# One weight load split over two DMA queues: the first 16 rows of w_in go to ScalarE's queue

## The chip, the core and the metric

The kernel runs on one core of one Trainium2 chip. The metric is device time in microseconds (us) of one execution. A core has five engines that run side by side: TensorE (PE, matrix products), VectorE (DVE), ScalarE (ACT), GpSimd (POOL) and SyncE (SP). SP, ACT and POOL can start DMA transfers, each on a queue of its own; the transfers of all queues are carried out by the same 16 DMA engines. Data is worked on in SBUF, a memory of 128 rows (partitions).

## What is computed

All data is fp32. With x of shape (2, 1, 512), the reference computes, cut to what matters:

```python
xn = layernorm(x)
# A: attention of one new token over the last W = 4096 of 32768 cached positions
q = (xn @ wq)                      # 512 -> 32 heads x 128
s = softmax(q k^T / sqrt(128)) v   # 8 key/value heads, each used by 4 query heads
s = s @ wo                         # 4096 -> 512
# B: a gated MLP
z = gelu(xn @ w_in)                # 512 -> 1792
h = z[:896] * (layernorm(z[896:]) * w_sp + b_sp)
g = silu(h @ w_out)                # 896 -> 512
out = x + s * g
```

With a batch of 2 and one token, nearly all the work is reading: 89.4 MB of weights and cache go through SBUF once.

## The kernel before

**Staging.** The large inputs arrive in tiles of 128 SBUF rows. w_in (512 x 1792) is laid out as 128 rows of 4 x 1792 numbers, so one SBUF row receives 28,672 contiguous bytes; w_out gives 14,336 bytes per row; each half of wq, and each of the eight k and eight v tiles (one per key/value head, both batch items), gives 32,768. The tile `win` (w_in), the two wq halves and all k and v tiles, later wo, share a ring of four slots (pool `ring`, function `slot`): a load into a slot has to wait until the tile that was there has been used. `wout` and the small tiles have space of their own.

**Queues.** Every large load is issued by SP, in the order w_in, w_out, wq, wq, k0, k1, v0, k2, v1 and so on up to wo. ACT's queue carries `xs` (x as 2 rows, for the layernorm), the two scalars w_sp and b_sp (tile `wb1`) and, at the end, the output. POOL's queue carries x once more, for the last addition. Instructions of each engine run in the order in which they are written (class `InOrder`); a planner adds the waits. It hands the completions of the SP and ACT transfers to eight semaphores in turn (called DMAHW0 to DMAHW7 below), so a transfer can also wait for the one that was issued eight places before it.

**Compute at the start.** `xs` goes through the layernorm (`st`, `mv`, `va`, `rs`, `xn`) on DVE and ACT, is transposed on TensorE and copied to `xnT`. Then 16 products (`z<-win,xnT`, in two passes each) need all of `win` and `xnT`. After them come the queries (`q_ps<-wq,xnT`), in four steps as wq arrives, with the rest of the MLP between them. From then on each head needs its k tile (transposed on DVE into `kt`, then the products `s`), and one head later its v tile (products `acc`). The last loads are wo, used by the products `part` and `so`.

The lines of most instructions read L37 in the profile, since a helper issues them; tiles tell them apart.

Of the kernel before, what the change touches and what calls it, by code (L numbers as in the profile page):

```python
# [14 lines left out]
P = 128  # L15
# [27 lines left out]
def kernel(  # L43
# [14 lines left out]
    pe, dve, act, sp = (InOrder(tc, e) for e in (nc.tensor, nc.vector, nc.scalar, nc.sync))  # L58
# [6 lines left out]
    F = w_in.shape[1]  # L65
    FH = F // 2
    KT = D // P
# [17 lines left out]
    def slot(name, *shape):  # L85
        return ring.tile([P, *shape], F32, tag="slot", name=name)
# [2 lines left out]
        return ps.tile([P, *shape], F32, tag="kt", name=name, bufs=3)  # L89


    xs = sb.tile([B, D], F32, tag="p", name="xs", bufs=1)
    act.dma_start(xs, x[:, 0, :])
    win_v = w_in.rearrange("(p k) f -> p k f", p=P)
    win = slot("win", KT, F)
    sp.dma_start(win, win_v)
    wout = big.tile([P, FT, D], F32, tag="wout", name="wout")
    sp.dma_start(wout, w_out.rearrange("(p j) d -> p j d", p=P))
    wq_v = wq.rearrange("(p k) f -> p k f", p=P)
# [32 lines left out]
    for n in range(HKV):  # L132
        p = Unit()
# [460 lines left out]
```

## Time and profile before

| | before |
|---|---|
| three timed runs, median (lowest to highest) | 217.18 us (216.87 to 217.79) |
| the profiled execution: span from the first to the last instruction | 214.9 us |
| median less that span | 2.3 us |
| read from HBM | 89.40 MB, 416 GB/s over the span |
| DMA queue of SP (q1) | 4032 packets, 89.39 MB, 96.9% of the 16 DMA engines' span |
| DMA queue of ACT (q10) | 20 packets, 0.01 MB |
| busy: PE, DVE, ACT, POOL | 64%, 49%, 11%, 2% |

The record gives the profiled execution no time of its own beside the span, so the span stands for it; the 2.3 us to the median of the timed runs lie around it. A packet is one piece of a transfer that one DMA engine moves without a break; for the large loads it is one SBUF row. In a table by stretches of time, a packet is counted, with its whole duration and its bytes, in the stretch in which it starts; so the DMA share of a short stretch can exceed 1.

### The profile page before, as it was taken

How to read it: one execution, taken by the hardware profiler on the slowest of the kernel's cores; microseconds unless marked ns; L12 is line 12 of the kernel's file. 1: busy time of each engine (PE TensorE's matmuls, PEld its weight loads, DVE VectorE, ACT ScalarE, POOL GpSimd, SP SyncE). 2: the span in 40 equal slices, each digit the busy share in tenths (PEclk: the TensorE clock that was granted, in tenths of full speed). 3: DMA queues.
4: the chain of work that ended last, by engine and by line, in shares of the span. 5: the costliest groups of instructions: out<-in, count | busy, mean ns of one | idle time of the engine just before them, and what ended most of it. 6: DMA issues, size and time to landing. Idle time of an engine off the chain costs nothing.

```text
span 214.9 us, 2108 instructions
## 1 busy us (share of the span) xinstructions
PE 138.0 (64%) x862; PEld 43.4 (20%) x862; DVE 104.9 (49%) x161; ACT 23.9 (11%) x60; POOL 4.0 (2%) x20
## 2 busy tenths in 40 slices
PE   0172193835865983992594199089467759989873
PEld 0120021212111221220121023033111113432321
DVE  2604014079549549529608910985784387240301
ACT  5003003110001011021021002012100011030110
POOL 7000000000000000000000000000000000000000
PEclk9997578896597698599599559959966757996998
DMA  7999999999999999999999999999999999999990
GB/s 257 428 439 445 433 433 445 401 451 415 451 427 427 442 415 451 409 457 421 439 430 433 445 415 445 415 451 424 421 451 421 451 409 450 415 418 418 427 401 36
DMA packets 4092, 89.52 MB, mean 417 GB/s; under 512 B 486, under 2 KB 498, under 8 KB 884
## 3 DMA queue, kind: packets, MB, share of 16 engines
q1 hardware_dynamic: 4032, 89.39, 96.9%
q8 instruction: 6, 0.10, 0.2%
q14 instruction: 2, 0.02, 0.0%
q10 hardware_dynamic: 20, 0.01, 0.0%
q0 software_dynamic: 32, 0.00, 0.0%
HBM read 89.40 MB, written 0.00 MB: 416 GB/s over the span
## 4 chain that ended last, share of the span: by engine, by line
DMA 69%; DVE 14%; PE 12%; ACT 1%; issue 1%; SPq 1%; ACTq 0%; DVEq 0%
DMA k<-in_A_k_cache_dram 33%; DMA v<-in_A_v_cache_dram 27%; DVE kt L37 11%; DMA wo<-in_A_wo_dram 9%; PE acc L37 5%; PE s L37 4%; PE pp L37 2%; ACT p L37 1%; DVE pT L37 1%; SPq L37 1%; DVE sm L37 1%; DVE qw L37 1%; DVE res L37 0%; PE so L37 0%; DVE mg L37 0%
## 5 line engine op out<-in xcount | busy, mean ns | idle before, releaser
L37 DVE STREAM_TRANSPOSE kt<-k 128x2048 f32<-128x2048 f32 x32 | 72.5, 2285 | 1.4 <-DMA k<-in_A_k_cache_dram 1.3
L37 PE MATMUL acc<-v,pT 128*32 128x512 f32 x256 | 42.6, 825 | 11.6 <-DMA v<-in_A_v_cache_dram 10.2
L37 PE MATMUL s<-kt,qw 128*32 128x512 f32 x256 | 40.3, 683 | 5.7 <-DVE kt L37 4.2
L37 PE MATMUL pp<-p,swap 128*128 128x512 f32 x16 | 12.6, 880 | 20.0 <-ACT p L37 20.0
L37 DVE CUSTOM_DVE_ANT_1 sm<-s,own 128x512 f32<-128x512 f32 x8 | 5.5, 691 | 35.8 <-PE s L37 35.7
L37 PEld LDWEIGHTS acc<-v,pT 128*32 128x32 f32 x256 | 10.7, 156 | 42.1 <-issue 32.0
L37 PE MATMUL q_ps<-wq,xnT 128*32 128x512 f32 x64 | 10.5, 785 | 12.0 <-DMA wq<-in_A_wq_dram 12.0
L37 PEld LDWEIGHTS s<-kt,qw 128*32 128x32 f32 x256 | 10.6, 121 | 33.8 <-issue 19.5
L37 ACT ACTIVATE o<-acc,diag 128x128 f32<-128x128 f32 x30 | 8.7, 367 | 62.6 <-PE acc L37 62.2
L37 ACT ACTIVATE p<-sm,nb 128x512 f32<-128x512 f32 x8 | 5.8, 722 | 77.8 <-DVE nb L37 77.8
L37 PE MATMUL col<-o,selw 128*32 128x128 f32 (+1 forms) x28 | 7.6, 439 | 0.9 <-DVE o L37 0.9
L37 DVE TENSOR_TENSOR lsum<-pl,diag 128x4 f32<-128x4 f32 x3 | 0.5, 162 | 15.7 <-PE pl L37 15.7
L37 PE MATMUL z<-win,xnT 128*32 128x448 f32 x32 | 5.0, 794 | 4.5 <-DMA win<-in_B_w_in_dram 4.5
L37 DVE STREAM_TRANSPOSE pT<-pp 128x512 f32<-128x512 f32 x8 | 5.7, 713 | 4.3 <-PE pp L37 4.3
L37 PEld LDWEIGHTS pp<-p,swap 128*128 128x128 f32 x16 | 3.0, 235 | 20.7 <-ACT p L37 20.7
L37 PE MATMUL mo<-mg,same 128*128 128x16 f32 x16 | 3.2, 273 | 5.8 <-DVE mg L37 5.3
L37 PE MATMUL part<-wo,oT 128*32 128x512 f32 x48 | 5.9, 598 | 0.1
L37 ACT ACT_TABLE_LOAD x4 | 5.1, 1283 | 2.0 <-issue 1.9
L37 PEld LDWEIGHTS q_ps<-wq,xnT 128*32 128x32 f32 x64 | 2.0, 126 | 15.5 <-DMA wq<-in_A_wq_dram 12.2
L37 PE MATMUL xnT_ps<-ident,xn 2*128 2x2 f32 x4 | 0.6, 252 | 6.9 <-DVE xn L37 6.9
L37 PEld LDWEIGHTS mo<-mg,same 128*128 128x128 f32 x16 | 2.4, 188 | 12.2 <-DVE mg L37 12.2
L37 DVE STREAM_TRANSPOSE zt<-z 128x448 f32<-128x448 f32 x1 | 1.0, 978 | 7.8 <-ACT z L37 7.8
(110 smaller groups left out, 62.4 us busy)
## 6 DMA issues: line engine op xcount, KB each, us to landing
k<-in_A_k_cache_dram SPq DMA_DIRECT2D x8, 4096.0 KB, 23.6
v<-in_A_v_cache_dram SPq DMA_DIRECT2D x8, 4096.0 KB, 31.4
wq<-in_A_wq_dram SPq DMA_DIRECT2D x2, 4096.0 KB, 28.8
wo<-in_A_wo_dram SPq DMA_DIRECT2D x2, 2048.0 KB
win<-in_B_w_in_dram SPq DMA_DIRECT2D x1, 3584.0 KB, 11.2
wo<-in_A_wo_dram SPq DMA_DIRECT2D x3, 1024.0 KB, 21.2
wout<-in_B_w_out_dram SPq DMA_DIRECT2D x1, 1792.0 KB, 15.0
wo<-in_A_wo_dram SPq DMA_DIRECT2D x1, 512.0 KB, 25.3
```

The lines of the kernel that those rows point to most:

```text
L37: return self.tc.keep_in_program_order(call(*args, **kwargs))
```

## The change

The load of `win` is cut into two transfers into the same tile: rows 0 to 15 on ACT's queue, as ACT's first instruction, and rows 16 to 127 on SP's queue, as SP's first. The load of `xs`, which was ACT's first, comes second there.

```diff
+    FIRST = 16
+    win_v = w_in.rearrange("(p k) f -> p k f", p=P)
+    win = slot("win", KT, F)
+    act.dma_start(win[:FIRST], win_v[:FIRST])
+    sp.dma_start(win[FIRST:], win_v[FIRST:])
     xs = sb.tile([B, D], F32, tag="p", name="xs", bufs=1)
     act.dma_start(xs, x[:, 0, :])
-    win_v = w_in.rearrange("(p k) f -> p k f", p=P)
-    win = slot("win", KT, F)
-    sp.dma_start(win, win_v)
     wout = big.tile([P, FT, D], F32, tag="wout", name="wout")
     sp.dma_start(wout, w_out.rearrange("(p j) d -> p j d", p=P))
```

ACT's instructions at the start of the program, before (16x7168 is 16 rows of 7168 numbers; `wb` is the tile of the two scalars, `rtx` a step of the layernorm):

```order
L37 DMA xs<-in_A_x_dram 2x512
L37 DMA wb_83<-in_B_w_sp_dram 1x1
L37 DMA wb_83<-in_B_b_sp_dram 1x1
L37 ACT_TABLE_LOAD
L37 ACTIVATE rtx<-va 2x1 [waits DVE_49]
```

and with the change:

```order
L37 DMA win<-in_B_w_in_dram 16x7168
L37 DMA xs<-in_A_x_dram 2x512
L37 DMA wb_84<-in_B_w_sp_dram 1x1
L37 DMA wb_84<-in_B_b_sp_dram 1x1
L37 ACT_TABLE_LOAD
L37 ACTIVATE rtx<-va 2x1 [waits DVE_49]
```

One DMA stands ahead of what was there; the rest keeps its order. SP's instructions at the start, before:

```order
L37 DMA win<-in_B_w_in_dram 128x7168
L37 DMA wout<-in_B_w_out_dram 128x3584
L37 DMA wq_79<-in_A_wq_dram 128x8192
L37 DMA wq_81<-in_A_wq_dram 128x8192
L37 DMA k_89<-in_A_k_cache_dram 128x1x8192
L37 DMA k_91<-in_A_k_cache_dram 128x1x8192 [waits DMAHW1_49,DMAHW0_49,PE_49]
```

and with the change:

```order
L37 DMA win<-in_B_w_in_dram 112x7168
L37 DMA wout<-in_B_w_out_dram 128x3584
L37 DMA wq_80<-in_A_wq_dram 128x8192
L37 DMA wq_82<-in_A_wq_dram 128x8192
L37 DMA k_90<-in_A_k_cache_dram 128x1x8192 [waits DMAHW0_49]
L37 DMA k_92<-in_A_k_cache_dram 128x1x8192 [waits DMAHW1_49,PE_49]
```

The order is the same. With one transfer more among those that take the eight semaphores in turn, k0 is now the ninth, and its issue waits for the first transfer (DMAHW0), where it waited for nothing.

## The prediction, made before the changed kernel was run

> **What bounds the kernel now.** I began with the share of the DMA engines and the chain of work that ended last, both on the page of the profile.
>
> ```profile
> DMA  7999999999999999999999999999999999999990
> q1 hardware_dynamic: 4032, 89.39, 96.9%
> DMA 69%; DVE 14%; PE 12%; ACT 1%; issue 1%; SPq 1%; ACTq 0%; DVEq 0%
> ```
>
> The DMA engines are busy in 38 of 40 slices; 96.9% of their time over the span is SP's queue. Is that a stream without holes, or does it starve and recover? The table by stretches answers (last two columns: share of the 16 DMA engines, GB/s):
>
> ```profile
> 40.00:100.00 60.00, 40.28 (x226) 11.38 (x216) 38.43 (x39) 6.23 (x17) 0.00 (x0) 0.80 1.00 431
> 100.00:150.00 50.00, 32.49 (x200) 10.84 (x202) 28.68 (x31) 5.05 (x16) 0.00 (x0) 0.76 1.01 433
> 150.00:190.00 40.00, 30.30 (x159) 8.88 (x151) 23.89 (x29) 2.77 (x8) 0.00 (x0) 0.79 1.00 431
> ```
>
> From 40 to 190 us the share is 1.00. The stream never waits for compute, so the time is: when the DMA engines start, plus bytes at 431 GB/s, plus whatever holds them up, plus the tail. The chain, in order of time, shows both ends:
>
> ```profile
> 2.74 43.47 DMA k<-in_A_k_cache_dram
> 191.50 19.59 DMA wo<-in_A_wo_dram
> 211.13 0.47 PE so L37 x8
> ```
>
> Until 46.2 us the chain is the queue ahead of k0; at the end the last wo arrives at 211.09 and 3.8 us of tail follow. So a lag that one DMA engine picks up in the first microseconds is still there when its last packet lands: nothing downstream absorbs it, since each engine has its own share of every tile and the last one decides. The change moves no other byte, so it is to be priced in the first 12 us, in steps of 0.1 us:
>
> ```profile
> 1.60:1.70 0.10, 0.00 (x0) 0.00 (x0) 0.00 (x0) 0.00 (x0) 0.10 (x1) 1.00 0.10 41
> 1.70:1.80 0.10, 0.00 (x0) 0.00 (x0) 0.00 (x0) 0.00 (x0) 0.10 (x1) 1.00 3.57 860
> 1.80:1.90 0.10, 0.00 (x0) 0.00 (x0) 0.00 (x0) 0.00 (x0) 0.10 (x1) 1.00 3.42 860
> 1.90:2.00 0.10, 0.00 (x0) 0.00 (x0) 0.00 (x0) 0.09 (x1) 0.07 (x1) 1.00 3.10 860
> 2.00:2.10 0.10, 0.00 (x0) 0.00 (x0) 0.00 (x0) 0.10 (x1) 0.04 (x1) 1.00 2.14 573
> 2.10:2.20 0.10, 0.00 (x0) 0.00 (x0) 0.00 (x0) 0.10 (x1) 0.10 (x1) 1.00 0.88 287
> 2.30:2.40 0.10, 0.00 (x0) 0.00 (x0) 0.00 (x0) 0.10 (x1) 0.10 (x2) 1.00 0.75 287
> 2.40:2.50 0.10, 0.00 (x0) 0.00 (x0) 0.10 (x1) 0.10 (x1) 0.10 (x2) 1.00 1.03 287
> 2.50:2.60 0.10, 0.00 (x0) 0.00 (x0) 0.10 (x1) 0.10 (x1) 0.10 (x2) 1.00 0.76 287
> 2.70:2.80 0.10, 0.00 (x0) 0.00 (x0) 0.10 (x2) 0.10 (x1) 0.10 (x2) 1.00 0.67 287
> 4.60:4.70 0.10, 0.00 (x0) 0.00 (x0) 0.00 (x0) 0.10 (x1) 0.10 (x2) 1.00 2.66 1147
> ```
>
> One row of w_in is 28,672 bytes; in a 0.1 us step that is 287 GB/s. So 860 means three packets started there, 573 two, 1147 four. The share times 0.1 us times 16 engines is the time that those packets took. Up to 2.8 us 3+3+3+2+1+1+1+1+1 = 16 packets start, one per engine: the sixteen engines start spread over 1.0 us. Their time is 16.32 x 0.1 x 16 / 16 = 1.63 us each, while at 4.6 us a packet takes 2.66 x 1.6 / 4 = 1.06 us. The earlier one starts, the slower: the first twelve take 13.11 x 1.6 / 12 = 1.75 us, the last one 0.67 x 1.6 = 1.07. So the pace of an equal packet depends on what moves beside it.
>
> **The change part by part.** *The start.* The issues stand at the same place:
>
> ```profile
> 0.74 0.37 SPq L37 DMA_DIRECT2D win<-in_B_w_in_dram  x1
> 0.75 0.56 ACTq L37 DMA_DIRECT2D xs<-in_A_x_dram  x1
> ```
>
> ACT issues only 0.01 us after SP, so its queue starts nothing earlier than 1.7 us; the small xs of the 1.60 step is the earliest that its queue did. What can be won is the spread: 16 rows are one packet per engine, and if every engine then starts at 1.75 instead of at a mean of 33.0 / 16 = 2.06 (middles of the steps above), 0.31 us are won on average, at most 1.0 for the engine that started last. I take 0.31.
>
> *The pace.* The 128-row load is the one shape whose steady pace the trace shows. The change replaces it by 16 neighbouring rows, written by all 16 engines at once, and by 112 rows in sevens. No large transfer of before has such a shape. Lower bound: each of an engine's 8 packets keeps 1.06 us, no loss. Upper bound: writers into neighbouring rows go one after another, 16 x 1.06 = 17.0 us for the 16 rows, 16 us lost. The only transfer into few rows is xs, 2 rows by two engines at once: share 0.10 x 1.6 / 2 = 0.08 us for 2,048 bytes, which is full pace (28,672 bytes at 1.06 would be 0.076 per 2,048). It speaks for the lower end, though 14 times smaller than a row of w_in. The nearest row with full-size packets that meet is the crowd of the first twelve, 1.75 us. I take that, between ends far apart, for all 8 packets of an engine: 8 x (1.75 - 1.06) = 5.5 us, of which 0.57 (1.63 - 1.06, the first packet's surplus) is paid already: **+4.9 us**.
>
> [...]
>
> *x behind 16 rows.* xs now waits behind one packet on its two engines. How a small packet fares beside SP's stream, the DMA lines show for 5.9 to 6.0 us:
>
> ```profile
> DMA packets 7, 0.09 MB, mean 871 GB/s; under 512 B 3, under 2 KB 4, under 8 KB 4
> q10 hardware_dynamic: 1, 0.00, 0.6%
> ```
>
> That is the first packet of the scalar w_sp, issued at 1.34. So beside a full SP queue ACT's may be served only after four of SP's packets. In that bad case: own row from 5.9 to 7.0, then SP, own completion, SP, x at about 9, its completion 10.2. Who waits:
>
> ```profile
> 2.69 0.67 DVE L37 BATCH_NORM_STATS2 st<-xs 2x6 f32<-2x512 f32 x1
> 7.64 0.17 DVE L37 COPY xnT<-xnT_ps 128x8 f32<-128x8 f32 x1 [0.86 <-PE xnT_ps L37]
> 12.03 4.29 PE L37 MATMUL z<-win,xnT 128*32 128x448 f32 x24 [4.50 <-DMA win<-in_B_w_in_dram]
> 17.13 0.54 SPq L37 DMA_DIRECT2D k<-in_A_k_cache_dram  x1
> 25.88 3.64 PE L37 MATMUL q_ps<-wq,xnT 128*32 128x512 f32 x16 [8.49 <-DMA wq<-in_A_wq_dram]
> 46.23 2.31 DVE L37 STREAM_TRANSPOSE kt<-k 128x2048 f32<-128x2048 f32 x1 [1.34 <-DMA k<-in_A_k_cache_dram]
> ```
>
> From bn_stats to xnT are 5.1 us. x from 2.7 to 10.2 puts xnT at 15.3 and z 3.3 us later than 12.0 (nothing if w_in itself comes 4.9 later). z frees the slot of k1, issued at 17.13; its bytes are not due before k0's are through at 46.2. A cover of some 29 us, and 8.5 us ahead of the queries; cost 0. DVE and ACT are idle in between, and behind ACT's extra issue (about 0.5 us, as xs now) stand only the small loads and a table load that the layernorm needs after x.
>
> *k0's new wait.* SP now holds k0's issue, at 2.74 before, until the 16 rows are in; behind it stands k1, which waits for z anyway. Ahead of k0 are 3.67 + 1.84 + 8.39 = 13.9 MB, 32 us at 431 GB/s. Even 17 us leave half of that; cost 0. Without that cover each us would count whole.
>
> *Sum.* Against the span of 214.9: -0.31 + 4.9 = +4.6, span 219.5; with 2.3 us around it, or 217.18 + 4.6, **221.8 us**.
>
> **The rivals.**
>
> *Nothing changes (217.0).* The two pieces together write the same bytes to each row, both beside each other; if engines seldom meet, the pace stays 1.06 and 0.2 to 0.3 us of start is all. For it: xs at full pace; 431 GB/s as a limit of the engines themselves, whatever the rows. Against: the 1.75 us of the first crowd.
>
> *Faster (215.6).* If the spread of starts costs the last engine its 1.0 us and the surplus of 0.57 comes from that ragged start, both go: 217.18 - 1.57. Against: the earliest starters are the slowest, so a common start should make the crowd larger.
>
> *Much slower (225.1).* Two engines share each way into SBUF during all of w_in: every packet takes 2 x 1.06, 8 x 1.06 = 8.5 us, less the 0.57 paid: +7.9. It decides once engines meet in pairs all the time. For it: all 16 rows are neighbours; against: sevens lie apart, and engines drift.
>
> *The change doesn't do what it says:* ACT's 16 rows are served after four SP packets, as the scalar was. Then they don't start the stream at all, the start's 0.31 is lost and the crowding comes later: 222.1, no other sign.
>
> **How the numbers follow.** About 0.5% (1.1 us) is what a measurement can tell from no change. Forecast, with its late-served form: 0.40 (its own range 218.5 to 224). Much slower: 0.20. Nothing: 0.31. Faster: 0.09. Slower by over 0.5%: 0.40 + 0.20 = 0.60; same 0.31; faster 0.09. Cases of both signs are open, so the range reaches from 216.3 (part of the start won) to 227.5 (the paired price and 2 us of drift), leaving out about 0.08 below and 0.1 above, where neighbours serialise further.
>
> **What would show it.** After the change, steps of 0.1 us should show all 16 first packets by about 2.0 us, and packets of 28.7 KB at 1.5 us or more until w_in is in; z starting at 16 to 17 us; k0's issue after the 16 rows, at no price; the stretches from 40 to 190 us again at a share of 1.00 with the same tail, and the last wo later by what w_in was late. If the early packets take 1.06 us, the forecast is wrong and it is the first rival; if xnT comes after w_in, and the stretches behind show holes, the cover was misjudged.

## The result, and the profile after

The changed kernel takes 226.01 us (median of six runs, 224.89 to 227.29) against 217.55 for the kernel before (216.87 to 218.21, six runs): a ratio of 1.0394, 95% interval 1.0366 to 1.0422. By the ratio it is 8.6 us slower (the medians differ by 8.5). The profiled execution's span grew by 9.3 us, from 214.9 to 224.2.

The page of the changed kernel, its DMA share, bytes per slice and queues:

```profile
DMA  9998999999999999999999999999999999999980
GB/s 174 206 240 304 445 438 462 392 455 421 427 456 409 444 447 403 438 456 403 450 418 438 450 409 438 462 398 447 427 421 456 415 438 449 409 409 428 424 351 11
q1 hardware_dynamic: 4016, 88.93, 95.3%
q10 hardware_dynamic: 52, 0.47, 1.3%
```

The share says the DMA engines are as busy as ever. The second line says what they deliver: in the first four slices (5.6 us each) 174 to 304 GB/s, from the fifth on about 430, until the stream ends. The share alone would have hidden the whole loss: a packet that crawls counts as busy.

The stretch from 1.5 to 20.5 us, of the kernel before and then of the changed one (last columns: DMA share, GB/s):

```profile
1.50:20.50 19.00, 5.96 (x38) 2.26 (x38) 6.87 (x30) 4.18 (x7) 3.26 (x14) 0.97 1.01 423
```

```profile
1.50:20.50 19.00, 0.61 (x4) 0.55 (x4) 4.19 (x20) 2.97 (x4) 3.25 (x14) 1.00 1.00 228
40.00:100.00 60.00, 40.32 (x234) 12.16 (x230) 36.32 (x48) 7.10 (x18) 0.00 (x0) 0.77 1.01 434
150.00:190.00 40.00, 30.10 (x162) 8.41 (x164) 26.71 (x23) 3.91 (x12) 0.00 (x0) 0.82 1.00 432
```

By 20.5 us the changed kernel has fetched (423 - 228) x 19 us = 3.7 MB less; at the 431 GB/s of the rest of the stream that is 8.6 us, as much as the timed difference. From 40 us on the rate is what it was. When w_in was whole, the issue lines tell (last column: us from issue to landing), of the kernel before and then of the changed one, for SP's piece:

```profile
win<-in_B_w_in_dram SPq DMA_DIRECT2D x1, 3584.0 KB, 11.2
```

```profile
win<-in_B_w_in_dram SPq DMA_DIRECT2D x1, 3136.0 KB, 20.3
```

Both were issued at 0.74, so the last row of w_in lands 9.1 us later. The end of the changed kernel's chain of waits:

```profile
200.71 19.46 DMA wo<-in_A_wo_dram
220.17 0.04 issue
220.22 0.47 PE so L37 x8
```

The last wo is issued at 200.71 instead of 191.50 and lands after 19.46 us instead of 19.59, with 4.0 us of tail instead of 3.8. So the 9.1 us by which w_in was late are 9.2 us at the last issue and 9.3 at the end: the lag of the first 20 us was carried through. The bytes give 8.6: they are a mean over the 16 engines, and a load is whole only when its last packet has landed.

Inside that stretch, first the kernel before from 1.5 to 10.6 us (queue: packets, MB, share of 16 engines), then the changed kernel from 1.5 to 17.9 us and, for ACT's 16 rows, from 3.0 to 6.5 us:

```profile
q1 hardware_dynamic: 128, 3.67, 99.8%
```

```profile
q1 hardware_dynamic: 110, 3.15, 82.4%
...
q10 hardware_dynamic: 16, 0.46, 84.0%
```

Before, the 128 packets of w_in took 0.998 x 9.1 x 16 / 128 = 1.14 us each. After, SP's took 0.824 x 16.4 x 16 / 110 = 1.97 us and ACT's 0.840 x 3.5 x 16 / 16 = 2.94 us. An engine has eight of them: 7 x 1.97 + 2.94 = 16.7 us instead of 9.1, 7.6 us more on average.

### The profile page after: what moved, and what is told of

It reads as the page before. It is cut to its first block, busy times and chain, and to the rows that moved or that the text cites. A ratio compares the mean times of both kernels' runs of the same rounds, so it can differ in the third digit from the quotient of the medians.

```text
span 224.2 us, 2109 instructions
## 1 busy us (share of the span) xinstructions
PE 135.2 (60%) x862; PEld 42.6 (19%) x862; DVE 105.0 (47%) x161; ACT 23.9 (11%) x60; POOL 4.0 (2%) x20
## 4 chain that ended last, share of the span: by engine, by line
DMA 73%; PE 13%; DVE 11%; ACT 1%; issue 1%; ACTq 0%; DVEq 0%
DMA v<-in_A_v_cache_dram 40%; DMA k<-in_A_k_cache_dram 19%; DMA wo<-in_A_wo_dram 9%; DVE kt L37 8%; PE acc L37 7%; DMA win<-in_B_w_in_dram 5%; PE s L37 3%; PE pp L37 2%; ACT p L37 1%; DVE pT L37 1%; DVE sm L37 1%; DVE qw L37 1%; DVE both L37 0%; PE col L37 0%; DVE res L37 0%
## 5 line engine op out<-in xcount | busy, mean ns | idle before, releaser
L37 PE MATMUL acc<-v,pT 128*32 128x512 f32 x256 | 39.0, 763 | 13.4 <-DMA v<-in_A_v_cache_dram 12.0
L37 PE MATMUL s<-kt,qw 128*32 128x512 f32 x256 | 38.6, 645 | 4.7 <-DVE kt L37 4.0
L37 PE MATMUL pp<-p,swap 128*128 128x512 f32 x16 | 13.9, 965 | 20.1 <-ACT p L37 20.1
L37 PEld LDWEIGHTS s<-kt,qw 128*32 128x32 f32 x256 | 9.2, 117 | 32.8 <-issue 19.4
L37 DVE BATCH_NORM_STATS2 st<-xs 2x6 f32<-2x512 f32 x1 | 0.7, 682 | 11.0 <-DMA xs<-in_A_x_dram 11.0
```

The source lines that it names most:

```text
L37: return self.tc.keep_in_program_order(call(*args, **kwargs))
```

## Experiments

Two theories stood against each other. **Rows**: a load is slow when it covers fewer than the 128 SBUF rows, by which rows it writes. **Queues**: two queues that take turns on each DMA engine, with x behind the larger one, slow each other.

### Both pieces on one queue

```diff
-    act.dma_start(win[:FIRST], win_v[:FIRST])
+    sp.dma_start(win[:FIRST], win_v[:FIRST])
```

> Both pieces of w_in, 16 rows and then 112, on SP's queue; x first on ACT's queue as before. Theory R (rows): a load into fewer than 128 SBUF rows is slow by its shape, whichever queue carries it: packets of w_in at about 2 us as in the changed kernel (229 GB/s from 12 to 16 us), z at 20 to 21 us, time within 1 us of the changed kernel's 226.0. Theory Q (queues): the loss comes from ACT's packets being interleaved with SP's on each DMA engine and from x behind them: w_in at 1.06 us per packet, z at about 12 us, 217.0 to 218.0.

Measured: 224.68 us, ratio 1.0349 (1.0326 to 1.0372). Its start:

```profile
1.50:20.50 19.00, 1.45 (x12) 0.90 (x16) 4.64 (x21) 2.97 (x4) 3.26 (x14) 1.00 1.00 252
19.66 5.61 PE L37 MATMUL z<-win,xnT 128*32 128x448 f32 x32 [11.97 <-DMA win<-in_B_w_in_dram]
```

With one queue and x early, 7.6 of the 8.6 us remain. The queue theory falls. The run came out a little faster than the row theory expected (225 to 227, z at 20 to 21 us). It also shows the 16 rows with no other large load beside them, since they are first in the queue; from 1.5 to 2.5 us:

```profile
q1 hardware_dynamic: 16, 0.46, 304.5%
```

That is 3.045 x 1.0 x 16 / 16 = 3.05 us a packet, where the first sixteen of the kernel before took 1.63. About 1 us less than in the changed kernel was measured, but the two intervals overlap, so what the second queue adds is not settled.

### Two queues, cut by columns

```diff
-    act.dma_start(win[:FIRST], win_v[:FIRST])
-    sp.dma_start(win[FIRST:], win_v[FIRST:])
+    LEFT = F * KT // 8
+    win_f, win_vf = win.rearrange("p k f -> p (k f)"), win_v.rearrange("p k f -> p (k f)")
+    act.dma_start(win_f[:, :LEFT], win_vf[:, :LEFT])
+    sp.dma_start(win_f[:, LEFT:], win_vf[:, LEFT:])
```

> w_in again on two queues in the same proportion, but cut by columns: the first 896 of the 7168 numbers of each of the 128 rows on ACT's queue ahead of x, the other 6272 on SP's. Every transfer covers 128 rows. Theory R: no loss, 217.0 to 218.0, a packet of 25,088 bytes at about 0.93 us; w_in read at 430 GB/s or more once under way. Theory Q: two queues still share each engine, and x still stands behind 8 packets: about 224 to 226.

Measured: 217.36 us, ratio 1.0014 (0.9994 to 1.0034): the same time as before.

```profile
1.50:20.50 19.00, 3.06 (x20) 1.33 (x24) 4.65 (x21) 2.97 (x4) 3.26 (x14) 1.00 1.02 420
12.86 0.68 DVE L37 BATCH_NORM_STATS2 st<-xs 2x6 f32<-2x512 f32 x1 [10.08 <-DMA xs<-in_A_x_dram]
18.05 5.85 PE L37 MATMUL z<-win,xnT 128*32 128x448 f32 x32 [0.33 <-DVE xnT L37]
```

Same split of bytes over the same two queues, 420 GB/s in the first 20 us. And x arrives 10 us late, so that z waits for xnT and starts 6 us later than before: that costs nothing. Two queues and a late x are both free; the shape is not. Nor does a second queue at the start win anything.

### x ahead of the 16 rows

```diff
+    xs = sb.tile([B, D], F32, tag="p", name="xs", bufs=1)
+    act.dma_start(xs, x[:, 0, :])
     FIRST = 16
...
     sp.dma_start(win[FIRST:], win_v[FIRST:])
-    xs = sb.tile([B, D], F32, tag="p", name="xs", bufs=1)
-    act.dma_start(xs, x[:, 0, :])
```

> As the changed kernel, but x is issued on ACT's queue ahead of the 16 rows. bn_stats again at about 2.7 us instead of 13.7. If x's lateness is hidden behind w_in (the prediction's cover), the time is 226.0 within 1; if a part of the loss is the late layernorm, 224 or less. z should start when w_in is in, at 19 to 21 us.

Measured: 226.52 us, ratio 1.0425 (1.0382 to 1.0469). bn_stats starts at 2.69 again, and z waits for w_in alone:

```profile
2.81 24.42 SPq L37 DMA_DIRECT2D k<-in_A_k_cache_dram  x2
7.65 0.17 DVE L37 COPY xnT<-xnT_ps 128x8 f32<-128x8 f32 x1 [0.87 <-PE xnT_ps L37]
21.15 5.49 PE L37 MATMUL z<-win,xnT 128*32 128x448 f32 x32 [13.62 <-DMA win<-in_B_w_in_dram]
```

xnT is ready 13 us before it is of use, and the time is that of the changed kernel within the intervals. k0 is issued at 2.81 here, against 11.37 in the changed kernel, where it waits for the 16 rows: that wait costs nothing either. The 16 rows are served later here than in the changed kernel; ACT's queue from 5.5 to 9.5 us:

```profile
q10 hardware_dynamic: 16, 0.46, 83.1%
```

They take 0.831 x 4.0 x 16 / 16 = 3.32 us each, so a later turn does not make them faster.

### The 112 rows alone

```diff
-    act.dma_start(win[:FIRST], win_v[:FIRST])
...
+    nc.gpsimd.memset(win[:FIRST], 0.0)
```

> The load of rows 0 to 15 is left out: those rows are set to zero, so the output lacks their part of x @ w_in; SP loads rows 16 to 127 and ACT's queue begins with x. 0.46 MB less is read, worth 1.06 us. Theory R: the 112 rows are slow by themselves, 7 packets at about 1.9 us instead of 1.06: about +5.5 against 217.5, 222 to 223.5, and the remaining 3 to 4 us of the loss belong to the 16 rows. Theory Q: without a second large queue, 1.06 us per packet, 216.5. If the 16 rows alone are the trouble, also 216.5.

Measured: 221.17 us, ratio 1.0191 (1.0154 to 1.0229), +4.2 us with 0.46 MB (1.06 us) less to read, so 5.2 us lost by the shape of 112 rows. Its DMA lines from 1.5 to 14.2 us:

```profile
q1 hardware_dynamic: 116, 3.24, 101.2%
q10 hardware_dynamic: 8, 0.00, 0.5%
```

By their bytes these are w_in's 112 packets, two of w_out and two of almost no bytes, at 1.012 x 12.7 x 16 / 116 = 1.77 us each (w_in's own a little more), with no other large load beside them. So the 112 rows are slow by themselves, as the 16 are in the run on one queue; the loss is a little under the 222 to 223.5 us expected. The 16 rows account for the remaining 226.0 - 221.2 = 4.8 us, 1.06 of it bytes.

### Sixteen more rows, placed differently

Now the kernel before, whole, with one load added: 16 rows of w_in once more, into the tile that k0 fills later. It stands at the head of ACT's queue, and x behind it. Only the rows change between the runs.

```diff
+    k0 = slot("k0", NT, DH)
+    act.dma_start(k0.rearrange("p t d -> p (t d)")[ROWS, : KT * F], win_v.rearrange("p k f -> p (k f)")[ROWS])
```

with ROWS = 0:16, then 0:112:7, then 0:128:8:

> The kernel before, with one load added: ACT's queue, ahead of x, reads the first 16 rows of w_in a second time into rows 0 to 15 of the tile that k0 later fills (nobody reads them; k0's load waits for it). The only large load of fewer than 128 rows. At full pace 0.46 MB cost 1.06 us: 218.5. If neighbouring rows crowd, 16 packets at about 2.9 us as in the changed kernel: +2.9, 220.3. The 128-row packets of w_in around them should be back at 1.06 us once the 16 are through.

> The same added load, same bytes, but of rows 0, 7, 14 and so on to 105, into the same rows of the tile. If the place of the rows is the cause, these 16 packets take 1.06 to 1.6 us: 218.5 to 219, against 220.3 for 16 neighbours. If 16 rows are slow because they are few, or because they stand on ACT's queue, the same 2.9 us and 220.3 again.

> The same added load with rows 0, 8, 16 and so on to 120. If only close neighbours crowd, as for every seventh row: about 1.06 us each, 218.5. [...]

Reading and writing were moved together in these, so two more kernels took them apart: from rows 0:16 of w_in into SBUF rows 0:112:7, and the reverse.

> The added 16-row load again, now from w_in's first 16 rows (458,752 contiguous bytes in HBM) into rows 0, 7, 14 to 105 of the tile. If the rows that are written (SBUF) are the cause, as with every seventh row on both sides: packets at about 1.5 us, 219 to 220. If the rows that are read (HBM) are, as with 16 neighbours on both sides: packets at about 3.3 us, 223.5 to 224.5.

> The counterpart: from every seventh row of w_in into rows 0 to 15 of the tile. If the rows written are the cause: about 3.3 us a packet, 223.5 to 224.5; if the rows read are: about 1.5 us, 219 to 220.

| read from rows | written to SBUF rows | ACT's packet, mean us | time us | ratio to before (95%) |
|---|---|---|---|---|
| 16 neighbours | 16 neighbours | 3.31 | 223.95 | 1.0281 (1.0228 to 1.0334) |
| every 7th | 16 neighbours | 3.00 | 221.91 | 1.0219 (1.0178 to 1.0261) |
| every 8th | every 8th | 2.02 | 220.10 | 1.0141 (1.0069 to 1.0213) |
| every 7th | every 7th | 1.53 | 219.71 | 1.0101 (1.0042 to 1.0161) |
| 16 neighbours | every 7th | 1.48 | 219.75 | 1.0124 (1.0098 to 1.0149) |

The packet means come from ACT's queue (16 packets each) in the DMA lines of these kernels, in the table's order and each from 3.0 to 7.5 us:

```profile
q10 hardware_dynamic: 16, 0.46, 73.5%
```

```profile
q10 hardware_dynamic: 16, 0.46, 66.7%
```

```profile
q10 hardware_dynamic: 16, 0.46, 44.9%
```

```profile
q10 hardware_dynamic: 16, 0.46, 34.1%
```

```profile
q10 hardware_dynamic: 16, 0.46, 33.0%
```

The first is 0.735 x 4.5 us = 3.31 us. The loads into neighbours were also served earlier, from 3 us on, than the others (from 5.4); but the kernel with x first has neighbours from 5.5 us on, beside the 112 rows, at 3.32 us a packet, and every 7th and every 8th row differ at the same turn. So the turn does not explain it. The same 0.46 MB, on the same queue, at the same place, takes 1.5 to 3.3 us a row, and what decides is **where it is written**: with the written rows fixed, other source rows change the packet by a tenth or less; with the source fixed, other written rows halve it. None of the five reaches the 1.06 us of the full-width load. In the times, every 7th and every 8th row are not told apart by their intervals, though the packets of the one profile of each are. From every 7th row into neighbours took 221.91 us where 223.5 to 224.5 were expected; the interval overlaps that of neighbours on both sides, so whether the rows read have a small share of their own is open.

Sixteen neighbours cost the whole kernel 6.1 us, more than expected (2.9). The expectation counted ACT's packets alone. But SP's packets beside them crawl as well; of that kernel SP's queue from 5.4 to 6.6 us, then the stretch from 1.5 to 20.5:

```profile
q1 hardware_dynamic: 7, 0.20, 155.2%
1.50:20.50 19.00, 2.35 (x16) 1.24 (x20) 4.53 (x21) 2.97 (x4) 3.26 (x14) 1.00 0.99 293
```

Seven packets of the 128-row load took 1.552 x 1.2 x 16 / 7 = 4.26 us each. (423 - 293) x 19 / 431 = 5.7 us, plus 1.06 for the added bytes: 6.8. The trace shows SP's packets slow beside the 16 neighbouring rows; in what way the one load slows the other it does not show.

### The cut in the middle

```diff
-    FIRST = 16
+    FIRST = 64
```

> The changed kernel with the cut at row 64: rows 0 to 63 on ACT's queue, 64 to 127 on SP's. If a load of fewer than 128 rows is slow whatever its number of rows, packets of about 2 us on both and 226, as in the changed kernel; if rows below and above 64 have ways of their own and engines at work on one half leave the other free, the two queues together run nearly at full pace, 218 to 220. x stands behind four packets: xnT later than w_in, at no cost by itself.

Measured: 226.14 us, ratio 1.0393 (1.0340 to 1.0446). DMA lines from 5.9 to 18.0 us:

```profile
q10 hardware_dynamic: 64, 1.84, 70.2%
q1 hardware_dynamic: 48, 0.92, 34.6%
```

ACT's 64 packets take 0.702 x 12.1 x 16 / 64 = 2.12 us. In which order the two queues were served is seen in shorter stretches; each line is all that SP's or ACT's queue started from 1.5 to 5.9 us, 5.9 to 7.9, 7.9 to 10, 10 to 12 and 12 to 14:

```profile
q1 hardware_dynamic: 32, 0.92, 97.4%
q10 hardware_dynamic: 16, 0.46, 104.4%
q1 hardware_dynamic: 16, 0.46, 100.5%
q10 hardware_dynamic: 16, 0.46, 103.9%
q1 hardware_dynamic: 16, 0.46, 103.2%
```

SP's queue holds rows 64 to 127 and ACT's rows 0 to 63, and the packets start in rounds of sixteen: two rounds of SP's, then ACT's and SP's by turns. So in each of these stretches the packets that started went to one half. SP's first 32 packets took 0.974 x 4.4 x 16 / 32 = 2.14 us each before ACT's began: 64 rows are slow by themselves, and two halves by turns do not make a whole. What two halves written at the same time would give is not tested by this kernel.

### One reading for all runs

The stretch from 1.5 to 20.5 us gives each run's price: (423 - GB/s) x 19 / 431, plus 1.06 us where 0.46 MB are added, minus it where they are left out. In the order of the table it was 228, 252, 225, 295, 420, 216, 293, 342, 390, 397 and 397 GB/s:

| kernel | from the stretch, us | from the timed ratio, us |
|---|---|---|
| the change | +8.6 | +8.6 |
| both pieces on one queue | +7.5 | +7.6 |
| x ahead of the 16 rows | +8.7 | +9.2 |
| 112 rows alone | +4.6 | +4.2 |
| cut by columns | +0.1 | +0.3 |
| cut in the middle | +9.1 | +8.6 |
| 16 neighbours added | +6.8 | +6.1 |
| every 7th row into neighbours | +4.6 | +4.8 |
| every 8th row added | +2.5 | +3.1 |
| every 7th row added | +2.2 | +2.2 |
| 16 neighbours into every 7th row | +2.2 | +2.7 |

The two columns agree within 0.7 us, with either sign, although the first comes from one profile of each kernel. So the first 20 us explain the losses to that accuracy.

## Why the prediction was right and wrong

**What held.** The bound: a stream without holes from 40 to 190 us, in which a lag of the first microseconds lasts to the end (9.1 us when w_in is whole, 9.3 in the span). The sign, and its reason: the two pieces have a shape whose pace the trace of before did not show, and it is slower (1.97 and 2.94 us a packet against 1.14). The covers: the late x (bn_stats at 13.7, even later than the bad case of 10.2) and k0's new wait cost nothing, shown by the kernel with x first (226.52 us against 226.01) and by the cut in columns (217.36 against 217.4). In the changed kernel xnT, ready at 18.9, still came before w_in:

```profile
13.72 0.68 DVE L37 BATCH_NORM_STATS2 st<-xs 2x6 f32<-2x512 f32 x1 [10.95 <-DMA xs<-in_A_x_dram]
18.69 0.17 DVE L37 COPY xnT<-xnT_ps 128x8 f32<-128x8 f32 x1 [0.87 <-PE xnT_ps L37]
21.17 5.00 PE L37 MATMUL z<-win,xnT 128*32 128x448 f32 x32 [2.59 <-DMA win<-in_B_w_in_dram]
```

**What failed: the size of one term.** The measured 226.0 us lie above the forecast of 221.8 and its own range (218.5 to 224). The step "for all 8 packets of an engine" at 1.75 us was mis-sized. It took the crowd of the first twelve packets as the nearest row. Measured were 1.97 us for SP's seven and 2.94 for ACT's one, a mean of (7 x 1.97 + 2.94) / 8 = 2.09. With it the term is 8 x (2.09 - 1.06) - 0.57 = 7.7 us where it stood at 4.9. The 0.31 us of the start did not come either (next paragraph), so the sum would have been +7.7. The 0.9 us to the measured 8.6 are not in these means; in the trace the last packet of w_in lands 9.1 us later. The first crowd was the wrong model, too: in the kernel before it has gone by 4.6 us, where a packet takes 1.06. The slow pace here lasts as long as the load (1.97 us a packet from 1.5 to 17.9 us), and for the 16 rows it is a matter of place (3.31 us into neighbours, 1.48 into every 7th row).

**The start.** The 0.31 us were not won. ACT's queue did not start the stream: the first 16 packets of the changed kernel, from 1.5 to 3.0 us, were all SP's:

```profile
q1 hardware_dynamic: 16, 0.46, 125.8%
```

They took 1.258 x 1.5 = 1.89 us each, where the first sixteen of the kernel before took 1.63. ACT's came after them. That is the rival in which the change does not do what it says: it came true beside the forecast, though after one round of SP's packets and not after four.

**The rivals.** "Much slower" named pairs that share a way into SBUF, 2 x 1.06 us for every packet, +7.9 us. That engines share one in pairs no run shows. In size this rival was the nearest of all, and the 64-row halves (2.12 us) and every 8th row (2.02) took close to that price. It was given half the chance of the forecast because sevens lie apart and engines drift; the 1.8 to 2.0 us a packet of the 112 rows show that this does not save them. The two small packets of x at full pace (0.08 us for 2,048 bytes), which spoke for the lower end, said nothing of rows of 28,672 bytes. "Nothing changes" is refuted by the 112 rows alone (1.77 us a packet), and "faster" by the start, whose sixteen packets became slower (1.89 us against 1.63).

**The place of the rows.** The runs show that the written rows decide: 3.31 and 3.00 us a packet into 16 neighbours, 2.02 into every 8th row, where 1.06 were expected if only close neighbours crowd, and 1.53 and 1.48 into every 7th. Why some rows are slow together no run shows.

**What stays open.** Which row of a 112-row load goes to which DMA engine isn't in the trace, and so why its packets take 1.8 to 2.0 us rather than another number is not shown. That the place of the written rows slows this load as well is concluded from the 16-row runs, not tested on 112 rows. The difference between the two neighbour runs (3.31 and 3.00 us) was not resolved.

## What to carry to other kernels

Cut a load by columns, not by rows, if it has to be cut: all 128 SBUF rows in each piece kept full pace here (217.36 us against 217.4, 420 GB/s in the first 20 us against 423), and 16 + 112 or 64 + 64 rows about halved it (228 and 216 GB/s). In a kernel that is one long stream, read the GB/s beside the DMA share, since slow packets look busy: the share was 1.00 at 228 GB/s here, 1.01 at 423. And price a transfer by a row of the same shape; where the trace has none, the upper price deserves as much weight as the near one.

## What the runs showed of the hardware

A load of 16 neighbouring SBUF rows slowed not only itself (3.31 us a packet) but the full-width load beside it (4.26 us a packet from 5.4 to 6.6 us, against 1.14): 0.46 MB cost 6.1 us, nearly six times what its bytes are worth at 431 GB/s. And ACT's load of 16 rows, issued within 0.01 us of SP's, started only after SP's first sixteen packets in the changed kernel (SP's from 1.5 to 3.0 us, ACT's from 3.3 on); in the five with a load added none of its packets started before 3.0 us. The small x of the kernel before, issued at the same 0.75 us, started at 1.6 us, ahead of SP's first packet at 1.7. With 16 neighbours on both sides the added packets started from 3.4 us on; with every 7th row on both sides, where ACT's issue itself took 0.63 us instead of 0.41, not before 5.4, after 48 packets of SP's:

```profile
0.75 0.41 ACTq L37 DMA_DIRECT2D k<-in_B_w_in_dram  x1
```

```profile
0.74 0.63 ACTq L37 DMA_DIRECT2D k<-in_B_w_in_dram  x1
```
